# An attention and Fourier-mixing kernel: all queues of its attention stages put into program order

## The chip, the cores and the metric

One Trainium2 chip, one core. The metric is device time in microseconds of one execution; the time of a kernel is the median of its runs. The profile is of one execution with the hardware profiler.

## What is computed

Four layers on a sequence of 2048 rows of 512 numbers, in fp32. Each adds to x what it computes of the LayerNorm of x:

```python
x = x + A(layernorm(x));  x = x + B(layernorm(x))
x = x + A(layernorm(x));  x = x + B(layernorm(x))

def A(x):                      # Fourier mixing, DFT matrices given
    a, b = x @ hid_re.T, x @ hid_im.T
    return seq_re @ a - seq_im @ b

def B(x):                      # 32 heads of 16, in 4 segments of 512 rows
    q, k, v = heads(x @ wq), heads(x @ wk), heads(x @ wv)
    for s in range(4):
        p = softmax(qs @ ks.T * scale + causal_mask)
        a_mem = (phi(qs) @ M) / (phi(qs) @ z + 1e-6)
        o = g * a_mem + (1 - g) * (p @ vs)
        M, z = M + phi(ks).T @ vs, z + sum(phi(ks))
    return concat(o) @ wo      # phi(t) = t + 1 if t > 0 else exp(t)
```

## The kernel before

The kernel has two spectral stages (A) and two attention stages (B) in turn. Wide products are exact to about fp32 by splitting each operand into a high and a low part (`split`: ACT rounds, DVE or POOL subtracts) and multiplying three times (`matmul3`, L91).

The whole program is written as Python generators that are placed in numbered slots (`place`, L160). A last loop (L878) runs through the slots in order and lets each generator that stands in a slot do one step; the number given to `place` orders the steps within a slot. TensorE (PE) issues its matmuls exactly in that order (`in_order`, L67). The instructions of the other queues, VectorE (DVE), ScalarE (ACT), GpSimd (POOL) and SyncE (SP), which issues nearly all DMAs, are put in order by the scheduler of the framework: it takes the ready instruction of the highest priority at the time that its own cost model gives. Two places raise a priority (`tc.high_priority`, L415 and L431). The order that it finds is fixed in the program; on the chip each queue runs its list from top to bottom and waits on semaphores.

An attention stage works in units of four heads of one segment (32 units per stage, ten slots each). For a unit there are:

- `natural_max` (L394): ten steps, each a matmul of scores (tile nat, q by k) into one PSUM bank, and DVE's row maximum over it with the mask (L416; tiles junk and mx). At the end four small steps split the maxima into three bf16 parts (mparts, L432 to L439), and `max_rows` (L445) puts them as three more rows under the transposed q (the stacked tile stkq) with a PE transpose, an ACT copy and a DMA on ACT's queue.
- `softmax_values` (L460): ten slots later the transposed scores (tile sT), now with the maximum taken off; ACT's Relu and Exp (L481, L482) write the weights pT, POOL zeroes the part above the diagonal (`causal`, L484), and 16 P·V matmuls (tile pv_bank) follow in the unit's slot 12.
- `output` (L562): four transposes, then on DVE a reciprocal (rec, L571), rec times the gate (L572) and two products (otmp, L588); from the second segment on POOL adds them to the result of the memory (L589).

For a group of eight heads (two units) there are `proj` (L314: twelve matmuls for q or k; then ACT's copy raw, POOL's cast and subtraction, ACT's second part, POOL's third, the store to DRAM from which `stack` loads the stacked operands; and for phi two ACT steps, L340 and L341, and a DVE sum, L345), `mem_read` (L594: from the second segment on; two steps, each four matmuls into a bank pm and on DVE a chain den, den, den, onat, L608 to L619, that reads it) and `mem_update` (L627; tile pM). For a row block there are `prep` (L278: load, statistics, LayerNorm, transposes) and `outproj` (L673).

All these PSUM tiles except pv_bank come from one pool of seven banks (`bank`, L102). The builder gives each tile its bank when it finds the order; a matmul into a bank waits until the last reader of the tile before has finished.

Of the kernel before, what the change touches and what calls it, by code (L numbers as in the profile page):

```python
# [18 lines left out]
P = 128  # L19
# [26 lines left out]
def spectral_infini_kernel(  # L46
# [13 lines left out]
    V, A, G, T = nc.vector, nc.scalar, nc.gpsimd, nc.tensor  # L60
# [14 lines left out]
    T = SimpleNamespace(matmul=in_order(T, "matmul"), transpose=in_order(T, "transpose"))  # L75
    half_neg = consts.tile([P, 1], F32, name="half_neg")
# [13 lines left out]

# [17 lines left out]
    def load_rows(src, name="xt"):  # L108
        t = sb.tile([P, 512], F32, name=name, tag="xt", bufs=6)
        nc.sync.dma_start(t, src)  # L110
        return t

    def load_split(dst, key, src, name, tag, bufs):
        raw = load_rows(src, "raw")
        yield
        dst[key] = w = pair(name, tag, bufs)
        split(w[:, 0], w[:, 1], raw)
        yield
# [17 lines left out]
    def layernorm(xt, mv, ve, r):  # L136
        t = sb.tile([P, 1], F32, name="rt", bufs=2)
        V.scalar_tensor_tensor(t, r, r, ve, op0=ALU.mult, op1=ALU.mult)
        V.tensor_scalar(t, t, -0.5, 1.5, op0=ALU.mult, op1=ALU.add)
        rr = sb.tile([P, 1], F32, name="rr", bufs=2)  # L140
        V.tensor_mul(rr, r, t)
        V.tensor_scalar(xt, xt, mv[:, 0:1], rr, op0=ALU.subtract, op1=ALU.mult)
        return xt

    def finish(ps, xr, x_out, i, **where):
        xo = sb.tile([P, D], F32, name="xo", **(where or {"bufs": 1}))
        V.tensor_tensor(out=xo, in0=ps, in1=xr, op=ALU.add)  # L147
        nc.sync.dma_start(x_out[i], xo)
        return xo

# [16 lines left out]
    def place_spectral(x_in, x_out, t0, ln_at, resident):  # L167
# [10 lines left out]
        def preload():  # L178
            pre.append(sb.tile([P, PRE, CP, 512], F32, name="cpre", tag="xT", bufs=1))
            for pc in range(PRE):  # L180
                for c in range(CP):
                    nc.sync.dma_start(pre[0][:, pc, c], ct[0, 0, pc, :, c])
                    yield

        def normalise(i):
# [7 lines left out]
            xn = layernorm(xt, *stats)  # L193
# [6 lines left out]
        def load_c(p, pc):  # L200
            if p == 0 and pc < PRE:
                raw = pre[0][:, pc]
            else:
                raw = pair("craw", "craw", 2, F32)
                nc.sync.dma_start(raw, ct[p % 2, p // 2, pc])
            yield
            hi, lo = pair("chi", "chi", 3), pair("clo", "clo", 3)
            with behind_first(p == 0 and pc == 0):
                split(hi, lo, raw)
            cs[p, pc] = (hi, lo)  # L210
# [22 lines left out]
        def hidden(tcn):  # L233
            for tt in range(LT):
# [14 lines left out]
                finish(ps, xr, x_out, tcn * LT + tt)  # L249
# [7 lines left out]
        for p in range(NP):  # L257
            for pc in range(NT // CP):
                t = kt(p, pc * CP)
                place(3, load_c(p, pc), [t - 10, t - (2 if p == 0 and pc < PRE else 4)])  # L260
            place(2, contract(p), [kt(p, i) for i in range(NT)])
        for k in range(2 * DT):
            c, d = k // DT, k % DT
            t = kt(1, k)
            place(3, load_split(wdt, (c, d), wd[c, d], "wdt", "wd", 8), [t - 3, t])
# [8 lines left out]
    def place_attention(x_in, x_out, t0, w_at, out_at, resident):  # L274
# [3 lines left out]
        def prep(s, i):  # L278
# [12 lines left out]
            split(xT[s][:, 0, :, sl], xT[s][:, 1, :, sl], pt)  # L291
            yield
# [21 lines left out]
        def proj(s, g, n):  # L314
# [32 lines left out]
            A.activation(raw, ps, AF.Copy, scale=sign)  # L347
            G.tensor_copy(parts[:, 0], raw)
# [11 lines left out]
            for a, cnt, step in SLOTS[n]:  # L360
# [3 lines left out]
                nc.sync.dma_start(dst[:, o : o + cnt], src)  # L364
# [9 lines left out]
        def stack(s, g, u):  # L374
            for n in "qk":
# [11 lines left out]
                nc.sync.dma_start(  # L387
# [57 lines left out]
        def max_rows(s, g, u):  # L445
# [9 lines left out]
            nc.scalar.dma_start(  # L455
# [4 lines left out]
        def softmax_values(s, g, u):  # L460
# [52 lines left out]
            for h in range(HU):  # L513

                def first(h=h):
# [3 lines left out]
                    if h % 2:  # L519
                        causal(p0[h // 2][:, :, :P])  # L520

                ev(6 + h, first)
            for h in range(HU):

                def second(h=h):
# [3 lines left out]
                    if h % 2:  # L529
                        for c in 0, 3 * P:  # L530
                            causal(p1[h // 2][:, :, c : c + P])
# [3 lines left out]
            for h in range(0, HU, 2):  # L535

                def third(h=h):
# [3 lines left out]
                    if h == 2:  # L541
                        causal(p2[0][:, :, :P])
# [19 lines left out]
        def output(s, g, u):  # L562
# [15 lines left out]
            for j in range(0, LT, 2):  # L578
# [5 lines left out]
                if s > 0:  # L584
                    if j == 0:
                        tmps = sb.tile([P, LT, HU, DH], F32, name="otmp", tag="ut", bufs=8)
                    tmp = tmps[:, j : j + 2]
                    V.tensor_tensor(out=tmp, in0=num, in1=rb, op=ALU.mult)  # L588
                    G.tensor_tensor(out=dst, in0=dst, in1=tmp, op=ALU.add)  # L589
                else:  # L590
                    V.tensor_tensor(out=dst, in0=num, in1=rb, op=ALU.mult)
            yield
# [68 lines left out]
        def transpose_out(s, i):  # L661
# [8 lines left out]
            split(t[:, 0], t[:, 1], pt)  # L670
            yield

        def outproj(s, i):  # L673
# [13 lines left out]
            if resident is not None and n in LAST:  # L687
                home = {"tag": "w", "bufs": 16} if s < NSEG - 1 else {"tag": "wd", "bufs": 8}
                resident[n] = finish(ps, xr, x_out, n, **home)
            else:  # L690
                finish(ps, xr, x_out, n)
# [15 lines left out]
        def outproj_split(s, i):  # L707
# [23 lines left out]
            finish(ps, xr, x_out, s * LT + i, tag="wd", bufs=8)  # L731
# [22 lines left out]
        for k in range(4 * DT):  # L754
            n, d = "qkvo"[k // DT], k % DT
            src = rows((wq, wk, wv, wo)[k // DT], d)
            place(3, load_split(ws, (n, d), src, f"w{n}", "w", 16), [w_at(k) - 3, w_at(k)])
# [7 lines left out]
        for s in range(NSEG):  # L765
            b = t0 + SS * s
            for i in range(LT):
# [3 lines left out]
                elif s == 1:  # L771
                    at = [b - 84 + 6 * i, b - 78 + 6 * i, b - 76 + 6 * i, b - 50 + (0, 2, 6, 8)[i]]
                else:
                    at = [b - 100 + 8 * i, b - 94 + 8 * i, b - 92 + 8 * i, b - 60 + (1, 2, 6, 8)[i]]
# [8 lines left out]
            if s == NSEG - 1 and x_out is out_tiles:  # L783
                for i in range(LT):
                    place(2, outproj_split(s, i), [o - 12 + i], range(o - 7 + 3 * i, o - 7 + 3 * i + 3), [o + 5 + 1, o + 7])
                place(1.5, transpose_last(s), [o + 5])
            else:
                for i in range(LT):
                    at = free[DT * i : DT * (i + 1)]
                    place(2, transpose_out(s, i), [at[0] - 4 - i % 2])  # L790
                    place(2, outproj(s, i), at)
            for g in range(NG):
# [9 lines left out]
                for n, k in ("q", 4), ("k", 8):  # L802
# [7 lines left out]
                    place(2, proj(s, g, n), at[k - 4 : k], [done + 1, done + 2, done + 3, last])  # L810
# [33 lines left out]
    def setup():  # L844
        nonlocal ident, ident_b, mask, same_head, gate
        with tc.issue_after(first_row[0].ins):
# [21 lines left out]
            nc.sync.dma_start(beta_b, beta[None, :].to_broadcast([P, H]))  # L868
# [55 lines left out]
```

## Time and profile before

| | us |
|---|---|
| median of 3 runs | 1954.03 |
| lowest and highest run | 1950.25, 1958.41 |
| the profiled execution, its own time | 1950.77 |
| its span, first to last instruction | 1949.10 |
| its attention stages, from the start of the span | 480 to 1000, 1440 to 1949 |

How the rows are read. A row of the timeline has start, length, engine, source line, operation and tiles (written <- read), and in brackets how long the engine had been idle and what ended that. A row of the waits has the waiting instruction, the one waited for, total us, how often, and the longest. A row of groups has busy time and mean nanoseconds of one instruction, then the idle time just before the group's instructions. A row of a stretch has its length and the busy time of PE, PEld (weight loads), DVE, ACT and POOL with the number of instructions, then the granted share of TensorE's clock, the share of the DMA engines, and GB/s. Lines of the source are those of the kernel before; every PE matmul has L71.

### The profile page before, as it was taken

To read this page: it belongs to the slowest core of one execution; us is meant where nothing else is said; L and a number is where in the kernel's file an instruction comes from. 1 tells how busy PE (TensorE), PEld (TensorE's weight loads), DVE (VectorE), ACT (ScalarE), POOL (GpSimd) and SP (SyncE) were. 2 spreads that over 40 slices of the span, in tenths; PEclk is the share of its full clock that TensorE was granted. 3 is DMA by queue.
4 is the path that set the end of the run, shared out by engine and by line. 5 is a ranking of instruction groups with operands and counts; after the bars stand their busy time and mean duration, and the time that the engine had idled before them with its cause. 6 is when DMAs were issued, how large, how long until landed. Compare 5 with 4: busy or idle time off the path is not lost. (4 is left out here: it accounts for less than half of the span.)

```text
span 1949.1 us, 30902 instructions
## 1 busy us (share of the span) xinstructions
PE 1849.3 (95%) x10528; PEld 1330.4 (68%) x10528; DVE 1111.8 (57%) x3665; ACT 956.7 (49%) x2026; POOL 523.0 (27%) x854
## 2 busy tenths in 40 slices
PE   7999999999899999998899999999998999999998
PEld 5788888887555655655478888888874556565554
DVE  8422222256777877867753222223567678777684
ACT  3312212142877777767732122121437777776775
POOL 6000000013443444445420000000234444434342
PEclk9999999999999999999899999999999999999999
DMA  6533332344433433435234332333444334344330
GB/s 189 168 98 98 98 97 87 105 149 153 148 114 99 153 109 116 139 107 179 79 104 134 92 103 87 108 95 98 154 155 145 115 97 150 117 131 131 96 121 34
DMA packets 122542, 231.41 MB, mean 119 GB/s; under 512 B 14352, under 2 KB 63504, under 8 KB 122384
## 3 DMA queue, kind: packets, MB, share of 16 engines
q1 hardware_dynamic: 119120, 228.65, 37.6%
q8 instruction: 83, 1.36, 0.3%
q10 hardware_dynamic: 3264, 0.79, 0.2%
q14 instruction: 75, 0.61, 0.1%
HBM read 161.50 MB, written 67.11 MB: 117 GB/s over the span
## 5 line engine op out<-in xcount | busy, mean ns | idle before, releaser
L71 PE MATMUL u<-chi,xh 128*128 128x512 f32 x2048 | 650.9, 392 | 10.5 <-ACT chi L83 9.5
L416 DVE CUSTOM_DVE_ANT_0 junk<-nat,mask 128x512 bf16<-128x512 f32 (+3 forms) x1024 | 497.3, 486 | 165.9 <-PE nat L71 142.9
L71 PEld LDWEIGHTS u<-chi,xh 128*128 128x128 f32 x2048 | 386.2, 189 | 92.7 <-ACT chi L83 9.5
L71 PE MATMUL u<-clo,xh 128*128 128x512 f32 x1024 | 400.3, 391 | 3.2 <-DVE clo L85 2.8
L85 DVE TENSOR_TENSOR clo<-craw,chi 128x1024 fp32r<-128x1024 f32 x124 | 153.1, 1236 | 421.9 <-ACT chi L83 421.4
L83 ACT ACTIVATE chi<-craw 128x1024 fp32r<-128x1024 f32 x124 | 131.2, 1059 | 531.5 <-PE u L71 512.8
L482 ACT ACTIVATE pT<-sT 128x512 f32<-128x512 f32 x640 | 366.5, 600 | 13.0 <-ACT sT L481 2.0
L485 POOL TENSOR_SCALAR_AFFINE_SELECT pT<-pT 128x256 f32<-128x256 f32 (+1 forms) x448 | 196.1, 452 | 370.0 <-ACT pT L482 350.9
L71 PE MATMUL nat<-stkk,stkq 96*128 96x512 bf16 (+3 forms) x1024 | 247.8, 303 | 33.4 <-DVE mx L416 28.4
L71 PE MATMUL sT<-stkq,stkk 99*128 99x256 bf16 (+3 forms) x1024 | 249.9, 308 | 21.3 <-DVE mx L416 15.9
L128 POOL TENSOR_TENSOR r<-ve,half_neg 128x1 f32<-128x1 f32 x64 | 41.4, 648 | 824.5 <-DVE ve L126 805.3
L481 ACT ACTIVATE sT<-sT 128x256 f32<-128x256 f32 (+1 forms) x640 | 205.4, 335 | 79.4 <-PE sT L71 71.3
L71 PEld LDWEIGHTS u<-clo,xh 128*128 128x128 f32 x1024 | 193.3, 189 | 44.2 <-DVE clo L85 3.2
L71 PE MATMUL y<-wdt,ut 128*128 128x512 f32 x768 | 196.6, 390 | 0.0
L71 PEld LDWEIGHTS <-stkk 99*128 99x128 bf16 x1024 | 78.9, 99 | 147.5 <-issue 133.7
L71 PEld LDWEIGHTS y<-wdt,ut 128*128 128x128 f32 x768 | 144.0, 188 | 30.1
L71 PE MATMUL pv_bank<-pT,vt 128*17 128x128 f32 (+3 forms) x2048 | 161.2, 444 | 1.8 <-POOL pT L485 1.8
L71 PEld LDWEIGHTS <-stkq 96*128 96x128 bf16 x1024 | 94.4, 99 | 94.2 <-issue 43.5
L71 PE MATMUL pqk<-xT,wq 128*128 128x512 f32 x384 | 131.1, 449 | 4.1 <-DVE xT L85 3.8
L71 PE MATMUL pqk<-xT,wk 128*128 128x512 f32 x384 | 129.1, 446 | 1.0 <-ACT pT L482 0.7
L71 PE MATMUL pvv<-wv,xT 128*128 128x512 f32 x384 | 128.2, 442 | 0.0
L71 PE MATMUL po<-wo,oh 128*128 128x512 f32 x384 | 122.0, 434 | 1.0 <-ACT oh L83 0.7
(107 smaller groups left out, 1944.7 us busy)
## 6 DMA issues: line engine op xcount, KB each, us to landing
craw<-in_ct SPq DMA_DIRECT2D x124, 512.0 KB
stkq<-scrq SPq DMA_DIRECT2D x64, 384.0 KB
stkk<-scrk SPq DMA_DIRECT2D x64, 384.0 KB
mid<-xo SPq DMA_DIRECT2D x48, 256.0 KB
scrq<-parts SPq DMA_DIRECT2D x32, 384.0 KB
scrk<-parts SPq DMA_DIRECT2D x32, 384.0 KB
xr<-mid SPq DMA_DIRECT2D x48, 256.0 KB
xt<-mid SPq DMA_DIRECT2D x40, 256.0 KB
```

Source lines behind the costliest of these rows:

```text
L71: return tc.keep_in_program_order(op(*args, **kwargs))
L83: A.activation(hi, src, AF.Copy, scale=scale)
L85: lo_engine.tensor_tensor(out=lo, in0=src, in1=hi.bitcast(F32), op=ALU.subtract)
L128: G.tensor_tensor(out=r, in0=ve, in1=half_neg, op=ALU.pow)
L416: V.tensor_tensor_reduce(junk[:, :n], src, mask[:, 512 - n :], 1.0, 3e38, ALU.add, ALU.min, dst,)
L481: A.activation(blocks, blocks, AF.Relu)
L482: A.activation(dst, ps, AF.Exp, scale=-SCALE)
L485: G.affine_select(blocks, blocks, pattern=[[0, n] for n in blocks.shape[1:-1]] + [[1, P]], compare_op=ALU.is_ge, fill=0.0, base=0, channel ...
```

## The change

The change wraps DVE, ACT, POOL and SP as TensorE is wrapped. While a flag is set, that is in all slots from 50 ahead of an attention stage to six behind its end, every instruction of these queues, DMA triggers too, keeps the order of the program; the raised priorities then have no effect there. Outside, the scheduler orders them as before.

So that an instruction that needs another engine doesn't stand straight behind the one that feeds it, steps are cut in two and the second half is placed one to three slots later: ACT's rounding and DVE's subtraction of a split (`split_steps`); POOL's cut of the diagonal one slot behind the Exp; POOL's addition of a unit's result one slot behind DVE's product; the store of a finished row block; the steps of `proj`, whose parts and store move from 1, 2, 3 to 1, 2, 3, 5 (first segment) or 1, 3, 4, 6 slots behind the last matmul. The sum for phi comes at least six slots behind it. LayerNorm follows its statistics by three slots in place of two. A row block that is kept for the next spectral stage is normalised into a new tile instead of in place.

```diff
+    strict = [False]
+    class InOrder:
...
+            def call(*args, **kwargs):
+                ins = op(*args, **kwargs)
+                return tc.keep_in_program_order(ins) if strict[0] else ins
...
+    V, A, G, Y = (InOrder(e) for e in (nc.vector, nc.scalar, nc.gpsimd, nc.sync))
...
+    def split_steps(hi, lo, src):
+        A.activation(hi, src, AF.Copy)
+        yield
+        V.tensor_tensor(out=lo, in0=src, in1=hi.bitcast(F32), op=ALU.subtract)
+        yield
...
-        V.tensor_scalar(xt, xt, mv[:, 0:1], rr, op0=ALU.subtract, op1=ALU.mult)
-        return xt
+        xn = xt if in_place else sb.tile([P, D], F32, name="xn", tag="xt", bufs=6)
+        V.tensor_scalar(xn, xt, mv[:, 0:1], rr, op0=ALU.subtract, op1=ALU.mult)
+        return xn
...
             A.activation(raw, ps, AF.Copy, scale=sign)
+            yield
             G.tensor_copy(parts[:, 0], raw)
...
-                        causal(p0[h // 2][:, :, :P])
+                        ev(7 + h, lambda: causal(p0[h // 2][:, :, :P]))
...
                     V.tensor_tensor(out=tmp, in0=num, in1=rb, op=ALU.mult)
-                    G.tensor_tensor(out=dst, in0=dst, in1=tmp, op=ALU.add)
+                    adds.append((dst, tmp))
...
+            yield
+            if s > 0:
+                for dst, tmp in adds:
+                    G.tensor_tensor(out=dst, in0=dst, in1=tmp, op=ALU.add)
...
-            place(1.9, output(*unit(n)), [t + 15 - (n + 1 == NSEG * USEG)])
+            place(1.9, output(*unit(n)), [t + 15 - last, t + 16 - last])
...
-                    at = [b - 100 + 8 * i, b - 94 + 8 * i, b - 92 + 8 * i, b - 60 + (1, 2, 6, 8)[i]]
+                    at = [b - 100 + 8 * i, b - 94 + 8 * i, b - 91 + 8 * i, b - 60 + (1, 2, 6, 8)[i]]
+                at.append(at[-1] + 1)
...
-                    place(2, proj(s, g, n), at[k - 4 : k], [done + 1, done + 2, done + 3, last])
+                    lag = (1, 2, 3, 5) if s == 0 else (1, 3, 4, 6)
+                    place(2, proj(s, g, n), at[k - 4 : k], [done + x for x in lag], [max(last, done + 6)])
...
     for t in sorted(slots):
         slots_done.append(t)
+        strict[0] = any(b - 50 <= t < b + LB + 6 for b in (b1, b2))
```

Every instruction of the wrapped queues has one source line in the changed kernel, L86.

The order of PE's matmuls is the same in both. What moves is seen best on DVE. First the unit with the memory read at the start of the second attention stage's last segment, in the kernel before (junk is a row maximum, otmp a product of `output`, den and onat the chain of `mem_read`, phi the feature sum of `proj`; the accumulator read behind each maximum is left out):

```order
L571 RECIPROCAL rec<-pv_bank 128x16
L416 ISA junk,mx<-nat,mask 128x128
L572 TENSOR_TENSOR rec<-rec,gate 128x16
L416 ISA junk,mx<-nat,mask 128x384
L588 TENSOR_TENSOR otmp<-pv_bank,rec 128x128 x2
L608 TENSOR_SCALAR den<-pm 128x16
L416 ISA junk,mx<-nat,mask 128x256
L609 RECIPROCAL den<-den 128x16
L345 SCALAR_TENSOR_TENSOR phi<-praw,phi 128x512
L416 ISA junk,mx<-nat,mask 128x512
L610 TENSOR_TENSOR den<-den,gate 128x16
L619 TENSOR_TENSOR onat<-pm,den 128x2x128
```

The same place in the changed kernel:

```order
L86 RECIPROCAL rec<-pv_bank 128x16
L86 TENSOR_TENSOR rec<-rec,gate 128x16
L86 TENSOR_TENSOR otmp<-pv_bank,rec 128x128 x2
L86 ISA junk,mx<-nat,mask 128x128
L86 ISA junk,mx<-nat,mask 128x384
L86 ISA junk,mx<-nat,mask 128x256
L86 TENSOR_SCALAR den<-pm 128x16
L86 RECIPROCAL den<-den 128x16
L86 TENSOR_TENSOR den<-den,gate 128x16
L86 TENSOR_TENSOR onat<-pm,den 128x2x128
L86 ISA junk,mx<-nat,mask 128x512
L86 SCALAR_TENSOR_TENSOR phi<-praw,phi 128x512
```

The chains of rec and den stand in one piece each, and phi has moved from ahead of the fifth step's maximum (128x512) to behind the eighth step's, one step ahead of the P·V matmuls.

The second place is LayerNorm on DVE. In the kernel before, several row blocks are handled together, interleaved, in one gap between two maxima, here in the second segment of the first attention stage (st, mv, ve: statistics; rt, rr, xt: normalisation):

```order
L141 TENSOR_TENSOR rr<-r,rt 128x1
L126 TENSOR_SCALAR ve<-mv 128x1
L122 BN_STATS st<-xt 128x6
L142 TENSOR_SCALAR xt<-xt,mv,rr 128x512
L138 SCALAR_TENSOR_TENSOR rt<-r,ve 128x1
L124 BN_AGGR mv<-st 128x2
L139 TENSOR_SCALAR rt<-rt 128x1
L416 ISA junk,mx<-nat,mask 128x256
```

In the changed kernel each row block's steps stand in their own slots, here the normalisation of one in a unit with a memory read:

```order
L86 TENSOR_SCALAR den<-pm 128x16
L86 RECIPROCAL den<-den 128x16
L86 TENSOR_TENSOR den<-den,gate 128x16
L86 TENSOR_TENSOR onat<-pm,den 128x2x128
L86 SCALAR_TENSOR_TENSOR rt<-r,ve 128x1
L86 TENSOR_SCALAR rt<-rt 128x1
L86 TENSOR_TENSOR rr<-r,rt 128x1
L86 TENSOR_SCALAR xt<-xt,mv,rr 128x512
L86 ISA junk,mx<-nat,mask 128x512
```

The statistics and the normalisation have moved later by some 37 maxima on the average, next to other work of DVE.

More of the change, by code (lines that the diff above doesn't have):

```diff
@@ L109, in load_rows @@
         t = sb.tile([P, 512], F32, name=name, tag="xt", bufs=6)
[L110 removed]
+        Y.dma_start(t, src)
         return t
@@ L116, in load_split @@
         dst[key] = w = pair(name, tag, bufs)
-        split(w[:, 0], w[:, 1], raw)
-        yield
+        yield from split_steps(w[:, 0], w[:, 1], raw)
     def row_stats(xt):
@@ L259, in place_spectral @@
                 t = kt(p, pc * CP)
-                place(3, load_c(p, pc), [t - 10, t - (2 if p == 0 and pc < PRE else 4)])
+                at = t - (2 if p == 0 and pc < PRE else 4)
+                place(3, load_c(p, pc), [t - 10, at, at + 1])
             place(2, contract(p), [kt(p, i) for i in range(NT)])
```

68 lines of the change are left out of this document (39 added, 29 removed).

## The prediction

> **What bounds the kernel now.** I read the page first, then the busy time by stage, then the waits of PE and DVE, then two stretches of one attention stage side by side.
>
> ```profile
> PE 1849.3 (95%) x10528; PEld 1330.4 (68%) x10528; DVE 1111.8 (57%) x3665; ACT 956.7 (49%) x2026; POOL 523.0 (27%) x854
> ```
>
> PE is busy 95% of the span: it is the bound, and the change can only win what PE idles. The stages say where that is (columns: stretch, its length, then busy time of PE, PEld, DVE, ACT, POOL):
>
> ```profile
> 0.00:480.00 480.00, 466.24 (x2046) 380.91 (x2046) 195.57 (x369) 121.20 (x157) 57.12 (x71) 1.00 0.40 126
> 480.00:1000.00 520.00, 477.54 (x3270) 298.48 (x3269) 388.09 (x1560) 368.70 (x872) 228.00 (x387) 0.96 0.39 120
> 1000.00:1440.00 440.00, 440.00 (x1955) 362.41 (x1953) 153.51 (x236) 105.40 (x134) 32.20 (x32) 1.00 0.37 115
> 1440.00:1949.10 509.10, 465.52 (x3262) 288.58 (x3261) 374.62 (x1502) 361.40 (x863) 205.69 (x364) 0.98 0.36 114
> ```
>
> The two spectral stages have no idle time worth the name (13.8 us at the start, 0.0 later). The two attention stages idle 42.5 and 43.6 us on PE, 86 us together, with DVE at about three quarters. So 86 us, 4.4% of the span, is the most that any reordering of the other queues can give. Whom PE waits for there (total us, times, longest; whole run):
>
> ```profile
> PE nat L71 <- DVE mx L416: 28.4, 32, 1.8
> PE sT L71 <- DVE mx L416: 15.9, 25, 1.4
> PE pm L71 <- DVE mx L416: 8.0, 9, 1.1
> PE pM L71 <- DVE mx L416: 5.7, 6, 1.1
> ```
>
> These four rows make 58.0 us. All end on the row-maximum step of DVE, and neither sT, pm nor pM uses its result: they wait for the PSUM bank that it reads. So the loss is DVE lagging behind PE while PE has only seven banks to run ahead in. It is not spread evenly. Here are two neighbouring units (four heads each) of the last segment, the first with a memory read (mem_read), the second without:
>
> ```profile
> 1819.93:1836.81 16.88, 14.37 (x103) 8.78 (x102) 12.54 (x50) 11.63 (x30) 9.73 (x15) 1.00 0.36 116
> 1836.81:1849.95 13.14, 13.14 (x95) 7.79 (x94) 8.99 (x41) 9.72 (x26) 4.01 (x10) 1.00 0.31 94
> ```
>
> Without the memory read PE never idles and DVE has 4.15 us to spare; with it PE idles 2.51 us. There are 24 such units. Inside the first one:
>
> ```profile
> 1823.62 0.25 DVE L571 RECIPROCAL rec<-pv_bank 128x16 f32<-128x16 f32 x1
> 1825.77 0.39 PE L71 MATMUL sT<-stkq,stkk 99*128 99x512 bf16 x1
> 1826.46 1.16 POOL L355 TENSOR_TENSOR parts<-rem,parts 128x512 bf16<-128x512 f32 x1
> 1826.64 1.53 DVE L345 SCALAR_TENSOR_TENSOR phi<-praw,phi 128x512 f32<-128x512 f32 x1
> 1826.92 0.39 PE L71 MATMUL sT<-stkq,stkk 99*128 99x512 bf16 x1
> 1828.83 0.38 PE L71 MATMUL nat<-stkk,stkq 96*128 96x128 bf16 x2 [1.52 <-DVE mx L416]
> 1830.07 0.42 DVE L619 TENSOR_TENSOR onat<-pm,den 128x256 f32<-128x256 f32 x1
> 1830.21 0.73 PE L71 MATMUL pm<-state,phi 128*128 128x136 f32 x4 [0.99 <-DVE mx L416]
> ```
>
> phi, which nobody needs for tens of us, runs 1.53 us in the middle of the burst; the chain that frees the first pm bank (den, den, den, onat) is cut up and ends only at 1830.49; PE stops twice, 1.52 and 0.99 us.
>
> **The change, part by part.** PE's own sequence of instructions is the same in both programs, and no arithmetic is added. So the sum has three terms: what the new order of DVE takes out of those waits, what it puts in, and what strictness costs at the start of each attention stage.
>
> (a) The burst. In the new order rec, rec, otmp stand in one piece, then four maxima, then the whole den chain, then the next maximum; phi stands behind the burst, just ahead of the P·V matmuls, during which DVE now waits:
>
> ```profile
> 1819.91 0.42 DVE L416 CUSTOM_DVE_ANT_0 junk<-nat,mask 128x256 bf16<-128x256 f32 x1 [2.63 <-PE nat L71]
> 704.65 0.69 DVE L345 SCALAR_TENSOR_TENSOR phi<-praw,phi 128x512 f32<-128x512 f32 x1
> ```
>
> That gap hides phi (0.69 us here, 1.53 above); if it were full, a phi would cost its 0.69 to 1.53 us each. I redo the unit by hand, from the first row of its fence, DVE at 1823.62. Durations: rec 0.25, rec times gate 0.43, two otmp 0.28 each, a maximum with its accumulator read 0.486 + 0.082 = 0.57, and the den chain uncut 1.12 (from 700.58 to 701.70):
>
> ```profile
> L416 DVE CUSTOM_DVE_ANT_0 junk<-nat,mask 128x512 bf16<-128x512 f32 (+3 forms) x1024 | 497.3, 486 | 165.9 <-PE nat L71 142.9 <-PE pv_bank L71 0.5
> L416 DVE DVE_READ_ACCUMULATOR2_ANT mx<- 128x1 f32 x1024 | 83.8, 82 | 0.0
> L572 DVE TENSOR_TENSOR rec<-rec,gate 128x16 f32<-128x16 f32 x64 | 27.7, 433 | 0.3
> L588 DVE TENSOR_TENSOR otmp<-pv_bank,rec 128x128 f32<-128x128 f32 x96 | 24.9, 281 | 0.3
> 700.58 0.17 DVE L608 TENSOR_SCALAR den<-pm 128x16 f32<-128x16 f32 x1 [0.60 <-PE pm L71]
> 701.28 0.42 DVE L619 TENSOR_TENSOR onat<-pm,den 128x256 f32<-128x256 f32 x1
> ```
>
> 1823.62 + 1.24 (rec to otmp) + 4 x 0.57 + 1.12 = 1828.26: the first pm bank is free, 2.2 us earlier than now. Three more maxima end at 1829.97. On PE the matmul nat that waited 1.52 us gets, by the built program's allotment of banks, that of the nat group before last, whose maxima are done by 1827.1: no wait at about 1827.2, 0.23 us behind the sT of 1826.92. The second pm stands in the first pm's bank: it would be due at 1827.4 and waits 0.9 us for 1828.26. The next nat is then due at 1829.7 and waits 0.3 us for 1829.97. In all 1.2 us in place of 2.51, so 52% of the wait goes. The allotment supports that for the other waits as well: 13 of 72 pm and pM tiles now stand in the bank of the matmul straight ahead, which is the pattern of the 15 waits of those two rows; in the new program none does. Of the 1280 nat and sT tiles 54 have less than 1 us of PE work between the bank's last use and theirs (57 waits in the rows), and in the new program 17. Applied to all four rows: 58.0 x 0.52 = 30 us gained. Bounds: nothing, if the same lag shows up elsewhere; 58 us, if all goes.
>
> (b) LayerNorm. The steps of the three later segments of each attention stage, 24 in all, now run mostly in gaps far ahead of their use; the new program pins them to their slots. One costs:
>
> ```profile
> L122 DVE BATCH_NORM_STATS2 st<-xt 128x6 f32<-128x512 f32 x56 | 38.3, 686 | 44.5 <-DMA xt<-mid 42.3 <-DMA xt<-in_x 2.2
> L142 DVE TENSOR_SCALAR xt<-xt,mv,rr 128x512 f32<-128x512 f32 x56 | 33.3, 595 | 0.8
> L138 DVE SCALAR_TENSOR_TENSOR rt<-r,ve 128x1 f32<-128x1 f32 x64 | 25.0, 391 | 25.7 <-POOL r L128 25.1
> L141 DVE TENSOR_TENSOR rr<-r,rt 128x1 f32<-128x1 f32 x64 | 12.5, 196 | 0.7
> L124 DVE BATCH_NORM_AGGREGATE mv<-st 128x2 f32<-128x6 f32 x64 | 11.1, 175 | 0.4
> L126 DVE TENSOR_SCALAR ve<-mv 128x1 f32<-128x1 f32 x64 | 9.4, 148 | 0.8
> L139 DVE TENSOR_SCALAR rt<-rt 128x1 f32<-128x1 f32 x64 | 9.3, 145 | 0.8
> ```
>
> Together 2.34 us. Most fall into units without a memory read, whose 4.15 us of spare DVE time hide them: nothing. In four units with one (two per stage) a statistics step and the previous row's normalisation stand inside the burst, where nothing hides them: 4 x 2.34 = 9 us lost. Bounds: 0, and 24 x 2.34 = 56 us if the spare time is taken by something else.
>
> (c) The start of each stage. The late features of segment 0 put ACT's two steps of 0.63 us (L340, L341) and DVE's sum in one slot, so DVE can stand 1.25 us with maxima queued behind it, eight times: 0 to 10 us. The split parts are stored one to three slots later, on the way to the first stacks: 0 to 5 us, from a slot of about 1.2 us (the sT of 1826.92 follows that of 1825.77 in 1.15). DVE's total wait for the feature is small now:
>
> ```profile
> L345 DVE SCALAR_TENSOR_TENSOR phi<-praw,phi 128x512 f32<-128x512 f32 x48 | 46.7, 973 | 3.1 <-ACT phi L341 3.1
> L340 ACT ACTIVATE phi<-praw 128x512 f32<-128x512 f32 x48 | 30.1, 626 | 0.7 <-ACT praw L347 0.5
> L341 ACT ACTIVATE phi<-phi 128x512 f32<-128x512 f32 x48 | 30.1, 627 | 0.1
> ```
>
> I take 2 us, near that row. The split steps, the stores and POOL's additions one slot later cost nothing: what reads them stands at least two slots on, and POOL is busy 27%.
>
> Sum: -30 + 9 + 2 = -19 us. The profiled execution took 1950.8 us, 1.7 more than its span, so 1931.8; it lies 3.2 below the median of the runs, 1954.0, so the forecast is **1935 us**.
>
> **Rivals.** First, no change: the maxima are as many, DVE must do the same 12.54 us in such a unit, and a lag that leaves one bank shows up at the next. For it: in the unit above DVE is the busiest engine behind PE. Against it: 16.88 - 12.54 = 4.34 us of the unit in which it isn't busy. If only the 13.7 us of pm and pM go, and those by half: -7 + 9 + 2, 1958 us.
>
> Second, slower: the queue's head. In strict order a step whose data is late holds every maximum behind it, and with them the banks. The candidates are the 24 LayerNorms (stage one, 500 to 980 us):
>
> ```profile
> DVE st L122 <- DMA xt<-mid: 10.1, 6, 3.1
> DVE rt L138 <- POOL r L128: 1.6, 4, 0.7
> ```
>
> Now six of them wait 1.7 us each. At 2 us for each of 24 this is 48 us: 1935 + 48 = 1983 us. It outweighs (a) from 30 - 9 - 2 = 19 us on, 0.8 us per LayerNorm. Against it: the loads stand six slots ahead, some 7 us.
>
> Third, port contention: DVE's phi took 1.53 us beside a POOL instruction of 1.16 us and 0.69 without. The new order puts q's phi into the slots of k's cast and subtraction on POOL. If all 48 met one, DVE had 48 x (1.53 - 0.97) = 27 us more work, and with the gap of 2.63 us already used by the backlog all of it would show: 1935 + 27 = 1962 us, no change by the bound below. The Trainium skill ("SBUF — State Buffer", Who interferes with whom) says that a VectorE instruction with two SBUF inputs and a GpSimd instruction that reads SBUF exclude each other for a whole instruction; the two phi rows agree with it. By that rule 1962 comes nearer; I keep the gap as cover.
>
> **Numbers.** About 0.5%, 9.8 us, can be told from no change. The forecast, with its range from all 58 us of (a) down to where it passes for no change (1902 to 1944): 0.58. No change (first rival 0.15, third 0.07): 0.22. Slower: 0.20. The low end is 1954 - 58 + 6 = 1902, all of (a) with half of (b) and (c); the high end, 1966, takes in the first and third rivals and leaves out most of the second.
>
> **What would show it.** Right: the four rows of PE waiting for mx fall from 58 to about 28 us, those of pm and pM change their releaser to onat; phi moves into the 2.6 us gap; PE's idle time in the two attention stages is about 67 us. Wrong: waits of PE for mx as long as before at other tiles (first rival); DVE rows st <- DMA or rt <- POOL above 30 us within the attention stages, with PE nat behind them (second); phi's mean well above 0.97 us with PE waiting (third). A rise of PE's waits for sT on stkq or stkk would show (c) mis-sized.

## The result, and the profile after

The changed kernel takes 2013.98 us (median of 4 runs, 2012.42 to 2015.14) where the kernel before takes 1954.17: ratio 1.0305, interval 1.0282 to 1.0328. It is 3% slower. Forecast were 1935 us and a range up to 1966, so both the sign and the range were wrong. The profiled execution has a span of 2013.4 us, 64.3 more than before.

By stage (columns as before), the two attention stages:

```profile
480.00:1030.00 550.00, 483.38 (x3254) 295.78 (x3253) 418.14 (x1592) 390.71 (x876) 230.51 (x392) 0.96 0.37 116
...
1470.00:2013.40 543.40, 485.67 (x3321) 298.25 (x3319) 405.23 (x1550) 385.05 (x871) 217.76 (x376) 0.98 0.37 115
```

PE now idles 66.6 and 57.7 us there, 124 in place of 86 (67 were forecast). Another 21 us of the 64 stand in PE's busy time, 1870.2 us for the same 10528 matmuls in place of 1849.3. Most of that goes with the stops. In a stream the end of one matmul lies under the start of the next: the sT of 1834.24 us is drawn 0.39 us long, and the next matmul starts 0.23 us behind its start. Ahead of a stop nothing covers that end. PE stops for more than 0.05 us 208 times in place of 129, and the uncovered ends make some 43 us in place of 28, an estimate, since the profile models the ends. The other 6 us stay open. Whom PE waits for in the whole run (total us, times, longest):

```profile
PE nat L71 <- DVE mx L86: 38.2, 51, 1.4
PE sT L71 <- DVE mx L86: 18.7, 26, 1.5
PE u L71 <- DVE xh L86: 7.9, 1, 7.9
PE sT L71 <- DMA stkq<-mt: 7.8, 2, 4.3
PE pm L71 <- DVE mx L86: 7.3, 6, 1.5
PE pm L71 <- DVE onat L86: 7.0, 12, 0.9
PE nat L71 <- DMA stkk<-scrk: 6.5, 2, 3.3
...
PE pM L71 <- DVE mx L86: 2.5, 5, 0.6
```

The four rows on mx make 66.7 us where 58.0 had been and 28 were forecast. Part of the forecast's picture is there: pm and pM wait 9.8 us for mx in place of 13.7, and pm waits for onat instead. But nat and sT wait 56.9 in place of 44.3. Three units show where. The first and the third have no memory read; the second is the unit that the prediction redid by hand:

```profile
1826.99:1842.95 15.96, 14.89 (x107) 9.47 (x106) 12.35 (x46) 10.52 (x26) 4.99 (x10) 1.00 0.53 167
1873.41:1889.12 15.71, 14.52 (x103) 8.85 (x102) 13.00 (x50) 11.98 (x29) 8.78 (x14) 1.00 0.33 101
1889.12:1902.92 13.80, 13.46 (x95) 7.80 (x94) 9.25 (x41) 10.65 (x27) 4.93 (x10) 1.00 0.38 117
```

The redone unit fell from 16.88 to 15.71 us; by hand, 1.2 us of waiting in place of 2.51, it was 15.57. PE waits 1.19 us in it, but not where the hand calculation had it:

```profile
1877.70 0.92 DVE L86 TENSOR_TENSOR rec<-rec,gate 128x16 f32<-128x16 f32 x1
1880.08 0.38 PE L71 MATMUL sT<-stkq,stkk 99*128 99x512 bf16 x1 [0.67 <-DVE mx L86]
1882.33 0.70 PE L71 MATMUL pm<-state,phi 128*128 128x136 f32 x4 [0.52 <-DVE onat L86]
```

rec times gate, beside a POOL subtraction of 1.16 us (rem, from 1877.43), took 0.92 us in place of the 0.43 in the sum; an sT that the sum didn't name waits 0.67 us for the maxima behind it; pm waits 0.52 us in place of 0.9, and the nat that was to wait 0.3 doesn't. The third unit rose from 13.14 to 13.80. The first, before, had no idle time on PE:

```profile
1773.54:1787.88 14.34, 14.34 (x107) 9.50 (x106) 10.51 (x45) 9.63 (x25) 3.89 (x9) 1.00 0.49 151
```

It grew by 1.62 us. DVE and the waits of PE at its beginning, after (the accumulator reads left out):

```profile
1827.79 0.69 DVE L86 TENSOR_TENSOR oh<-oT,oh 128x512 fp32r<-128x512 f32 x1
1828.39 0.16 DVE L86 SCALAR_TENSOR_TENSOR mparts<-mx 128x16 bf16<-128x16 f32 x1
1828.56 1.16 POOL L86 TENSOR_TENSOR parts<-rem,parts 128x512 bf16<-128x512 f32 x1 [3.52 <-ACT parts L86]
1828.59 1.16 DVE L86 SCALAR_TENSOR_TENSOR mrem<-mx,mparts 128x16 f32<-128x16 f32 x1
1829.67 0.16 DVE L86 SCALAR_TENSOR_TENSOR mparts<-mx,mparts 128x16 bf16<-128x16 f32 x1
1829.87 0.26 DVE L86 SCALAR_TENSOR_TENSOR mparts<-mrem,mparts 128x16 bf16<-128x16 f32 x1
1830.05 0.68 DVE L86 CUSTOM_DVE_ANT_0 junk<-nat,mask 128x512 bf16<-128x512 f32 x1
1830.79 0.38 PE L71 MATMUL nat<-stkk,stkq 96*128 96x128 bf16 x2 [0.44 <-DVE mx L86]
...
1831.84 0.98 PE L71 MATMUL po<-wo,oh 128*128 128x512 f32 x3 [0.61 <-DVE mx L86]
```

For 2.26 us, 1827.79 to 1830.05, no maximum runs: oh and the four steps of mparts and mrem stand ahead of it in one piece, mrem stretched to 1.16 us beside POOL. PE runs into the banks of the late maxima at 1830.79 and 1831.84. DVE had its spare time in that unit, but later, beside the P·V matmuls (2.51 us idle up to the maximum at 1842.93).

All units together, each from its first nat matmul to that of the next, from the timelines of four kernels (two of them experiments below), in us. The last unit of all has no next one and is counted to its own last nat matmul, in the first row; without it that row falls by 8.5 us from before to after:

| | before | after | projection's cut alone (e5) | after, DVE's chains free (f4) |
|---|---|---|---|---|
| 23 units with a memory read | 394.2 | 388.5 | 352.6 | 363.0 |
| 22 units without, in later segments | 309.7 | 346.2 | 312.6 | 329.6 |
| 18 units of the first segments | 273.1 | 284.1 | 264.2 | 274.9 |
| last unit of the first attention stage, and the spectral stage behind it | 481.0 | 497.5 | 483.1 | 498.6 |

The groups behind two of the rivals, in the changed kernel:

```profile
L86 DVE SCALAR_TENSOR_TENSOR phi<-praw,phi 128x512 f32<-128x512 f32 x48 | 42.2, 879 | 1.5 <-ACT phi L86 1.5
L86 DVE BATCH_NORM_STATS2 st<-xt 128x6 f32<-128x512 f32 x56 | 38.3, 686 | 2.3 <-DMA xt<-in_x 2.3
L86 DVE SCALAR_TENSOR_TENSOR rt<-r,ve 128x1 f32<-128x1 f32 x64 | 23.2, 363 | 6.8 <-POOL r L86 6.8
```

The waits of st for its rows (42.3 us before) and of rt for POOL (25.7 us of idle time before) are all but gone, and phi is a little shorter. So the loss is in none of them. In the table above, the units with a memory read gained only 5.7 us; those without, costed at nothing, lost 36.5; the first segments and the transition lost 27.5.

### The profile page after: what moved, and what is told of

Same layout as the page of the kernel before. It is cut to its first block, busy times and chain, and to the rows that moved or that the text cites. A ratio compares the mean times of both kernels' runs of the same rounds, so it can differ in the third digit from the quotient of the medians.

```text
span 2013.4 us, 30670 instructions
## 1 busy us (share of the span) xinstructions
PE 1870.2 (93%) x10528; PEld 1333.8 (66%) x10528; DVE 1149.6 (57%) x3665; ACT 995.4 (49%) x2026; POOL 529.8 (26%) x854
## 4 chain that ended last, share of the span: by engine, by line
PE 71%; DVE 21%; issue 4%; ACT 3%; DMA 1%; POOL 0%; SPq 0%; DVEq 0%; ACTq 0%; POOLq 0%
PE u L71 33%; DVE junk L86 9%; PE y L71 8%; PE pv_bank L71 8%; PE pqk L71 6%; PE nat L71 4%; PE sT L71 4%; PE po L71 3%; PE pvv L71 3%; DVE rec L86 2%; ACT pT L86 1%; DVE st L86 1%; PE pM L71 1%; DVE xt L86 1%; DVE rt L86 1%
## 5 line engine op out<-in xcount | busy, mean ns | idle before, releaser
L86 DVE CUSTOM_DVE_ANT_0 junk<-nat,mask 128x512 bf16<-128x512 f32 (+3 forms) x1024 | 500.4, 489 | 211.3 <-PE nat L71 160.9
L86 DVE TENSOR_TENSOR clo<-craw,chi 128x1024 fp32r<-128x1024 f32 x124 | 156.9, 1266 | 434.2 <-ACT chi L86 434.2
L86 ACT ACTIVATE chi<-craw 128x1024 fp32r<-128x1024 f32 x124 | 131.3, 1059 | 533.8 <-PE u L71 511.8
L86 ACT ACTIVATE pT<-sT 128x512 f32<-128x512 f32 x640 | 382.4, 598 | 24.2 <-ACT sT L86 0.4
L86 POOL TENSOR_SCALAR_AFFINE_SELECT pT<-pT 128x256 f32<-128x256 f32 (+1 forms) x448 | 197.3, 454 | 393.9 <-ACT pT L86 353.9
L86 POOL TENSOR_TENSOR r<-ve,half_neg 128x1 f32<-128x1 f32 x64 | 40.5, 633 | 834.5 <-DVE ve L86 804.2
L86 ACT ACTIVATE sT<-sT 128x256 f32<-128x256 f32 (+1 forms) x640 | 214.6, 335 | 61.7 <-PE sT L71 45.4
```

Source lines behind the costliest of these rows:

```text
L86: ins = op(*args, **kwargs)
```

## Experiments

Medians are of 4 to 10 runs each; the kernel before stood at 1953 to 1955 us beside them. "Cuts" are the steps cut in two and placed later, "strict" is a queue kept in the order of the program.

**Cuts without strictness (e1), and one queue or group strict at a time (e2, e3).**

```diff
-        strict[0] = any(b - 50 <= t < b + LB + 6 for b in (b1, b2))          # e1
-                return tc.keep_in_program_order(ins) if strict[0] else ins
+                return tc.keep_in_program_order(ins) if strict[0] and self.engine is nc.vector else ins      # e2
+                return tc.keep_in_program_order(ins) if strict[0] and self.engine is not nc.vector else ins  # e3
```

> The change without the flag: all steps cut and placed as in the changed kernel, but the scheduler orders DVE, ACT, POOL and SP everywhere. Theory Q (a queue's head: in strict order an instruction that waits for another engine holds what stands behind it; the cuts alone do nothing, since a scheduler that is free to reorder passes them by): within 10 us of the kernel before, 1944 to 1964 us. Rival C (the cuts themselves cost: results come one to three slots later, and stacks, transposes and stores with them): at least half of the 60 us stays, 1985 us or more. Rival B (bursts: DVE's chains kept in one piece): as Q here.

> Only DVE keeps the order of the program; ACT, POOL and SP are free. Theory Q: the waits of ACT's first instruction (xh behind xt, 15 us for eight in the first attention stage) go, as the scheduler sets other work ahead of them, so of the 60 us some 30 go: 1975 to 1990 us. Rival B (DVE's own order, LayerNorm in one piece among the maxima, makes the loss): 2000 to 2014 us. A third, that DVE's order gains as forecast and all the loss is ACT's: 1935 to 1955 us.

> Only ACT, POOL and SP keep the order of the program; DVE is free and its maxima have their raised priority again. Theory Q: ACT's xh still stands ahead of Relu and Exp and waits for DVE's xt, so a good part of the 60 us stays: 1975 to 1995 us. Rival B (DVE's order alone): 1945 to 1960 us.

Measured: e1 1907.33 us, ratio to before 0.9761 (0.9746 to 0.9775). e2 1973.72. e3 1991.11. The last two are about where theory Q put them. No theory had the first: the cuts alone gain 47 us, so strictness costs not 60 but 107 us, with DVE alone 66 and with the others alone 84. Wherever DVE is free its scheduler sets statistics early, and DVE stands for their rows: 44.5 us before, 44.3 in e1, 51.2 in e3. So that wait is hardly a part of the 84, which is counted from e1. In the changed kernel it is 0 apart from the program's start.

**ACT's xh two slots behind DVE's xt (e4).**

```diff
+            early = t0 > 0 and i < 12
...
             xn = layernorm(xt, *stats, in_place=i not in LAST or not t0)
+            if early:
+                yield
             xh[i] = pair("xh", "w", 16)
-            place(3, normalise(i), ... [t - (8 if i < 12 else 4), t - 3, t])
+            place(3, normalise(i), ... [t - 8, t - 5, t - 2, t] if t0 and i < 12 else [t - (8 if i < 12 else 4), t - 3, t])
```

> The changed kernel with one more step cut, that of the second spectral stage's LayerNorm: DVE's xt comes two slots ahead of ACT's xh and of POOL's part in place of the same slot (twelve row blocks in the last six units of the first attention stage). Those units and the transition to the spectral stage lost 29.5 us against before. Theory Q: the row ACT xh <- DVE xt falls from 14.7 us below 4, and 15 to 25 us of the 29.5 come back: 1989 to 1999 us. Rival B (it is DVE's LayerNorm among the maxima that costs there, which stays): 2009 to 2016 us.

Measured: 2010.88 us, 3 less. The row in the whole run, first in the changed kernel, then in e4:

```profile
ACT xh L86 <- DVE xt L86: 33.7, 21, 3.3
```

```profile
ACT xh L86 <- DVE xt L86: 20.6, 15, 3.3
```

It fell by 13 us for a gain of 3, so this head of ACT's queue isn't what costs, and theory Q failed in the form that it had here.

**One cut alone (e5), and one step of it alone (g1).** e5 is the kernel before with the projection's cut:

```diff
             A.activation(raw, ps, AF.Copy, scale=sign)
+            yield
             G.tensor_copy(parts[:, 0], raw)
...
-                    place(2, proj(s, g, n), at[k - 4 : k], [done + 1, done + 2, done + 3, last])
+                    lag = (1, 2, 3, 5) if s == 0 else (1, 3, 4, 6)
+                    place(2, proj(s, g, n), at[k - 4 : k], [done + x for x in lag], [max(last, done + 6)])
```

g1 is the kernel before with this alone:

```diff
+            yield
+            A.activation(parts[:, 1], rem, AF.Copy)
             if with_phi and not late:
                 feature()
-            yield
-            A.activation(parts[:, 1], rem, AF.Copy)
```

> The kernel before with one cut of the change alone, that of the projection: ACT's copy one step ahead of POOL's cast and of the two feature steps, and parts and store 1, 2, 3, 5 or 1, 3, 4, 6 slots behind the last matmul. Nothing is strict. The cuts together gained 47 us, most of it in the 24 units with a memory read (16.89 us in place of 14.7 in the plain ones). Theory P (the gain is the feature sum phi, 0.97 us a piece on DVE and 0.74 with the cuts, that no longer stands among the maxima of those units): 1954 less 35 to 50, 1905 to 1920 us. Rival S (the gain comes from several cuts, LayerNorm and the splits among them): 1930 to 1950 us.

> The kernel before with ACT's two feature steps alone placed one slot later, behind ACT's second part; nothing is cut, nothing strict. DVE's sum phi of the units with a memory read then stands some eleven instructions later on DVE, about where the projection's cut puts it. Theory P (phi's place among the maxima is the gain of the cuts): 1903 to 1920 us. Rival S (the later cast, parts and store of the projection are needed too): 1935 to 1955 us.

Measured: e5 1903.02 us, ratio 0.9731 (0.9713 to 0.9749), just beyond theory P's range, faster than both kernels and the best of all runs. g1 (only the two ACT steps of the feature moved behind ACT's second part) 1925.91, ratio 0.9859 (0.9843 to 0.9874), between the two ranges. The unit that the prediction redid, and the one behind it, in e5:

```profile
1777.09:1791.77 14.68, 14.34 (x103) 8.87 (x102) 11.37 (x50) 11.67 (x30) 9.64 (x15) 1.00 0.43 135
1791.77:1804.91 13.14, 13.14 (x95) 7.79 (x94) 8.99 (x41) 9.72 (x26) 3.85 (x9) 1.00 0.30 92
```

PE idles 0.34 us in place of 2.51. DVE in the burst (behind L347, e5's line numbers are one higher than those of before):

```profile
1785.29 0.56 DVE L417 CUSTOM_DVE_ANT_0 junk<-nat,mask 128x384 bf16<-128x384 f32 x1
1785.78 0.17 DVE L609 TENSOR_SCALAR den<-pm 128x16 f32<-128x16 f32 x1
1785.98 0.25 DVE L610 RECIPROCAL den<-den 128x16 f32<-128x16 f32 x1
1786.15 0.70 DVE L345 SCALAR_TENSOR_TENSOR phi<-praw,phi 128x512 f32<-128x512 f32 x1
1786.78 0.16 DVE L611 TENSOR_TENSOR den<-den,gate 128x16 f32<-128x16 f32 x1
1786.87 0.68 DVE L417 CUSTOM_DVE_ANT_0 junk<-nat,mask 128x512 bf16<-128x512 f32 x1
```

The chain of den is still cut up, but phi comes two nat steps later than before (here ahead of the seventh step's maximum) and takes 0.70 us in place of 1.53. Over all, and in g1:

```profile
L345 DVE SCALAR_TENSOR_TENSOR phi<-praw,phi 128x512 f32<-128x512 f32 x48 | 35.3, 736 | 4.7 <-ACT phi L341 4.7
```

```profile
L345 DVE SCALAR_TENSOR_TENSOR phi<-praw,phi 128x512 f32<-128x512 f32 x48 | 44.8, 932 | 27.7 <-ACT phi L341 27.7
```

phi's place is the gain in the units with a memory read: g1 moves nothing but the feature's steps and what the scheduler then reorders around them; it takes 14.78 us for the redone unit and has 27 of e5's 51 us. Against e5 it is 11 us longer in the units with a memory read, 13 in the first segments and a little shorter elsewhere. Two things differ that may make this, and neither was tested alone: in g1 DVE waits 27.7 us for ACT at phi (4.7 in e5), and phi's mean is still 0.93 us (0.74).

**What of DVE's order costs: LayerNorm or the short chains (e6, f1, f2, f4).** In each, only some instructions are left to the scheduler, the others keep their order among themselves:

```diff
+                if not (self.engine is nc.vector) or not strict[0] or loose[0]:   # e6, f1, f2; f4: all queues
+                    return ins
...
+            loose[0] = True     # f1, f2, f4, up to loose[0] = False: around rec, rec, otmp; den, den, den, onat; mparts, mrem
+            V.reciprocal(rec, pn[:, :, :, DH])
...
+        loose[0] = True         # e6, f2: around row_stats and layernorm
```

Left to the scheduler, the steps of mparts and mrem have their raised priority again, too.

> The cuts, with DVE alone in the order of the program as in the run with only DVE strict (1973.7 us), but LayerNorm's instructions (statistics, the root on POOL, the normalisation) left to the scheduler; the rest of DVE keeps its order. Theory L (LayerNorm pinned into its slots is the greater part of the 66 us that DVE's strict order costs beside the cuts alone, 34 us in units 2 to 19 and 34 to 51 and some 20 in the last units of the first stage): 1915 to 1930 us. Rival B (it is every chain in one piece, rec, den and mparts too, that holds the maxima): 1945 to 1974 us.

> The cuts, DVE alone in the order of the program (1973.7 us), but its short chains left to the scheduler: rec, rec times gate and the two products of output; den, den, den, onat of the memory read; the four steps that split the maxima. LayerNorm and the rest keep their order. Theory B (a chain in one piece holds the maxima behind it by 0.6 to 1.2 us, in every unit; in the cuts alone the scheduler sets one link between two maxima): 1920 to 1935 us. Theory LB (chains and LayerNorm each fill the lag that the other leaves, so freeing one alone gives nothing, as freeing LayerNorm gave nothing): 1960 to 1974 us.

> As the run with DVE's chains left to the scheduler, and LayerNorm left to it too; the maxima and the other steps of DVE keep their order. Theories B and LB: 1905 to 1920 us, near the cuts alone (1907.3). If it stays above 1940, the order of the maxima against the remaining steps of DVE (sums, splits, features) is what costs.

> The changed kernel, all four queues strict (2014.0 us), but DVE's short chains left to the scheduler as above. Theory B: DVE's part of the loss goes, some 23 us, to where the run with ACT, POOL and SP strict stood: 1985 to 1995 us. Theory LB: 2005 to 2014 us.

Measured: e6 1972.65 us, 1.1 less than e2: theory L fails. f1 1931.37, 42 less than e2, as theory B had it. f2 1931.17, so LayerNorm gives 0.2 with the chains free as well: theory LB fails. The 24 us between f2 and the cuts alone are less than that run's third case had named; only the order of the maxima against DVE's other steps is left to make them. f4 1967.03, ratio to before 1.0064 (1.0048 to 1.008): 47 us less than the changed kernel, twice what theory B had forecast for it. The three units of the fences above, in f4:

```profile
1786.58:1801.23 14.65, 14.58 (x107) 9.49 (x106) 11.25 (x46) 10.35 (x26) 5.04 (x10) 1.00 0.52 168
1831.86:1846.67 14.81, 14.09 (x103) 8.80 (x102) 12.07 (x50) 11.79 (x29) 8.78 (x14) 1.00 0.35 107
1846.67:1860.46 13.79, 13.51 (x95) 7.79 (x94) 9.77 (x41) 10.65 (x27) 4.99 (x10) 1.00 0.38 117
```

And the beginning of the first of them on DVE, the same steps as in the fence of the changed kernel:

```profile
1787.37 0.69 DVE L86 TENSOR_TENSOR oh<-oT,oh 128x512 fp32r<-128x512 f32 x1
1787.98 0.16 DVE L86 SCALAR_TENSOR_TENSOR mparts<-mx 128x16 bf16<-128x16 f32 x1
1788.06 0.68 DVE L86 CUSTOM_DVE_ANT_0 junk<-nat,mask 128x512 bf16<-128x512 f32 x1
1788.67 0.67 DVE L86 SCALAR_TENSOR_TENSOR mrem<-mx,mparts 128x16 f32<-128x16 f32 x1
1789.26 0.16 DVE L86 SCALAR_TENSOR_TENSOR mparts<-mx,mparts 128x16 bf16<-128x16 f32 x1
1789.35 0.28 DVE L86 CUSTOM_DVE_ANT_0 junk<-nat,mask 128x128 bf16<-128x128 f32 x1
```

One maximum now stands behind oh and the first link, at 1788.06, where the changed kernel held it for the whole chain; in that unit PE no longer waits for DVE. The 128x512 maximum starts 0.69 us after oh began in place of 2.26.

**What of the other queues' order costs (e7, e8, g2), and two tries at ACT's (f3, g3).** e7 and e8 set the flag for ACT alone, and for POOL and SP alone; g2 is f4 with ACT free; f3 is e7 with one ACT step free; g3 is f4 with other slots:

```diff
+            loose[0] = True                                              # f3
             A.activation(parts[:, 1], rem, AF.Copy)
+            loose[0] = False
...
-                    lag = (1, 2, 3, 5) if s == 0 else (1, 3, 4, 6)       # g3
+                    lag = (1, 2, 3, 5) if s == 0 else (1, 2, 3, 6)
```

> The cuts, with ACT alone in the order of the program. ACT, POOL and SP strict together cost 84 us beside the cuts alone (1907.3). Theory A (ACT's order costs most of it: Relu and Exp in turns instead of two and two, and steps that wait for PE or DVE ahead of them): 1960 to 1990 us. Rival X (the waits are those of POOL and of SP's transfers): 1907 to 1930 us.

> The cuts, with POOL and SP in the order of the program, DVE and ACT free. Theory A: 1907 to 1930 us. Rival X: 1960 to 1990 us. If both engines share the loss, this run and the one with ACT alone lie near 1950 us each.

> The cuts, ACT alone in the order of the program (1957.0 us), but ACT's second part of a projection left to the scheduler. In strict order it comes later, POOL's third part (1.16 us) then runs beside DVE's mrem, whose mean was 0.49 us there and 0.20 with the cuts alone, and PE waits for the maxima behind it. Theory N (that neighbourhood of DVE and POOL is a good part of the 50 us that ACT's order costs): mrem's mean back below 0.25 us and 1920 to 1940 us. Rival A (Relu and Exp in turns, and what stands at the head of ACT's queue): 1950 to 1957 us.

> DVE (its short chains left to the scheduler), POOL and SP strict, ACT free. With ACT strict as well it was 1967.0 us. Theory A (ACT's order is the greater part of what is left): 1920 to 1940 us. Rival X (the waits only move to POOL or DVE): 1955 to 1967 us.

> All four queues strict, DVE's short chains free (1967.0 us), and from the second segment on the second and third part of a projection one slot earlier, 1, 2, 3, 6 slots behind the last matmul in place of 1, 3, 4, 6, so that POOL's third part no longer stands in the slot in which DVE splits the maxima. Theory N (the two engines meet there: mrem 0.39 us in that run and 0.20 with the cuts alone, some 0.74 us of PE in a plain unit): mrem's mean below 0.25 us and 1945 to 1957 us. Rival A (the waits at the head of ACT's queue are what costs): 1964 us or more, slower if ACT now waits for POOL at each projection.

Measured: e7 1957.03 us, 50 above the cuts alone and just short of theory A's range. e8 1931.41, 24 above, so neither extreme holds; ACT's share is twice that of POOL and SP. g2 1938.22, as theory A had it: with DVE's chains free, ACT's order is worth 29 us. f3 1995.86, worse by 39 and outside both its ranges. g3 1967.74, no gain, in rival A's range. The rows of mrem, e7, f4 and g3 in turn:

```profile
L86 DVE SCALAR_TENSOR_TENSOR mrem<-mx,mparts 128x16 f32<-128x16 f32 x64 | 31.4, 491 | 0.1
```

```profile
L86 DVE SCALAR_TENSOR_TENSOR mrem<-mx,mparts 128x16 f32<-128x16 f32 x64 | 25.0, 391 | 0.0
```

```profile
L86 DVE SCALAR_TENSOR_TENSOR mrem<-mx,mparts 128x16 f32<-128x16 f32 x64 | 14.2, 222 | 0.0
```

Both f3 (0.20 us) and g3 took the collision away, and the units that it had lengthened came back: the plain unit ahead of the redone one takes 15.09 us in e7, 14.35 in f3; 15.08 in f4, 14.35 in g3. Since ACT's Relu and Exp still alternate in f3 and g3, their turns cost nothing there. But other units grew. In f3 the redone unit went from 14.93 to 17.49 us:

```profile
1868.20 0.63 ACT L86 ACTIVATE parts<-rem 128x512 bf16<-128x512 f32 x1 [1.03 <-POOL rem L86]
1875.14 0.38 PE L71 MATMUL sT<-stkq,stkk 99*128 99x256 bf16 x2 [2.02 <-DMA stkq<-mt]
```

The freed step now stands ahead of mt on ACT's queue and waits there for POOL, 46.6 us over the run in place of 13.8. The DMA that ACT issues behind mt is late, and PE waits for it 25.7 us over the run in place of 8.6. So this head of ACT's queue does cost. phi's mean rose as well, from 0.71 to 1.04 us. In g3 some units with LayerNorm grew, one of them from 15.20 to 17.65 us: POOL's third part (1.17 us) had moved there from mrem to LayerNorm's xt, which took 1.46 us in place of 0.55. So theory N is right on the mechanism and wrong on the sum.

**The flag ends early (g4).** `t < b + LB - 70` in place of `t < b + LB + 6`, otherwise f4:

> All four queues strict, DVE's short chains free (1967.0 us), and the flag ends 70 slots ahead of the end of each attention stage instead of six behind it, so that the last units of each stage and the way into the next are free. Theory E (the end of the stages, where rows for the next stage are normalised and the last maxima are late, is a good part of what is left: the last six units and the transition of the first stage stood 20 us above the cuts alone): 1940 to 1952 us. Rival (the loss is spread over all units): 1955 to 1962 us.

The flag then leaves out the last seven units of each stage. Measured: 1949.80 us, 17 less than f4, as theory E had it. The stretch from the last unit of the first attention stage through the spectral stage falls from 498.6 to 483.8 us (481.0 before).

## Why the prediction was wrong, step by step

- **PE's sequence, and where the loss can be.** PE's order is the same, and what moved the time is PE's stops in the attention stages and at their ends. But the 86 us of idle time were no upper bound: PE's busy time moves with the stops, 1833.3 us in e5, 1849.3 before, 1870.2 after.
- **The burst, -30 us: this step failed.** The total of its hand-worked unit came out (15.57 forecast, 15.71 measured), with luck: the waits lie at other tiles, and an sT's 0.67 us that was not in the sum stands in for what pm and nat did not wait. What failed is "52% of the wait goes", carried over to all four rows, and the reason behind it, that rec, otmp and den "in one piece" free the banks sooner. The 23 units with a memory read gained 5.7 us. The gain in the redone unit is phi's leaving the burst, which the projection's cut brings by itself (51 us over the run, 14.68 us for the unit; with the feature's steps alone 27 and 14.78). The chains in one piece work against it: left to the scheduler, they give 47 us in the changed kernel and the redone unit takes 14.81. The hand calculation saw the sum of both and credited the chains as well as phi.
- **"Whose 4.15 us of spare DVE time hide them: nothing": failed for the units, if not for LayerNorm.** Leaving LayerNorm free gains nothing (e6, f2), so as far as tested the cover held for it. But the sum took the units without a memory read at nothing altogether, and spare time over a unit was no cover for steps at its beginning. These units, with the same chains of `output` and mparts ahead of their maxima, lost 36.5 us; leaving the chains to the scheduler (f4) gives 16.6 of that back, and 19.9 stay with the rest of the order. I had costed the chains only where PE already waited.
- **LayerNorm, +9 us.** Nearer than its upper bound of 56, and too high: with DVE alone strict, leaving it to the scheduler gives 1.1 and 0.2 us, no more than the runs of one kernel differ. With all four queues strict it wasn't tried.
- **Start of each stage, +2 us.** Mis-sized: the first unit of each stage takes 17.03 us in place of 15.46, and ahead of it PE waits 3.3 and 3.2 us for stkk where it did not wait before. That is some 10 us, inside the bounds of 0 to 15. The waits of sT for stkq, 7.8 us in place of 4.0, are in the last unit of each stage and not at its start.
- **The split steps, stores and POOL's additions at nothing.** The cuts cost nothing, they gain. What I had not costed at all is that ACT, POOL and SP are strict too: with DVE's chains free, ACT's order is 29 of the 60 us left to the cuts alone, and 17 of the 60 fall in the last units of the stages.
- **Rivals.** The second had the sign and not the place: st waits 0 us for its rows in the attention stages and rt 6.8 for POOL in the whole run in place of 25.1. The pinned order does that and not the three slots alone: e1 has them too, and there st stands 41.8 us and rt 22.4. What holds the maxima is mostly not late data at the head of DVE's queue but work whose data is there. The first, a lag that shows up at the next bank, is the nearer one: the rows moved from pm and pM to nat and sT. The third found DVE and POOL in each other's way, but at mrem and rec rather than at phi (mean 0.88 us, 0.97 before); in the redone unit phi still took 1.50 us beside POOL, in the gap that was to cover it.
- **Open.** The losses don't add up: DVE's 66, ACT's 50 and the 24 of POOL and SP make 140 beside the cuts alone, together they cost 107. Of ACT's 29 us only the collision at mrem was shown, and taking it away in g3 gave nothing net, since POOL then met LayerNorm; what makes the rest was not found.

## What to carry to other kernels

Before a queue is put into a fixed order, look at which of its instructions frees a buffer that the bound engine waits for, and count what stands ahead of it in every unit, not only in the units that wait now; spare time later in the unit didn't help here. Split a change into its parts and time each: here one cut gained 51 us and the order that it was made for cost 107. A hand calculation that hits the total of one unit hasn't shown which of its terms made it.

## What was not expected of the hardware

A DVE instruction of 128x16 elements, mrem, took 1.16 us beside a POOL addition of 1.16 us that had begun 0.03 us earlier; its mean is 0.18 us in the kernel before, 0.24 in the changed kernel and 0.49 in e7, where the two meet regularly. The Trainium skill ("SBUF — State Buffer", Who interferes with whom) states that a VectorE instruction with two SBUF inputs contends with a GpSimd instruction that reads SBUF, for ports that one of them holds alone. The trace agrees: mrem reads mx and mparts, and ends with the POOL instruction, however short it is by itself.
